# Linear attention and a leaky-ReLU MLP on one core: the two MLP products by one level of Strassen's method

## The chip, the cores and the metric

The kernel runs on one NeuronCore of a Trainium2 chip. The core has a matrix engine (TensorE, PE in the profile; its weight loads are PEld), VectorE (DVE), ScalarE (ACT), GpSimd (POOL) and SyncE (SP), which here issues the loads. Each engine has its own list of instructions and waits for others by semaphores. The metric is the device time of the core in microseconds (us), lower is better.

## The reference, cut to what matters

```python
# q, k, v: (8, 8, 576, 64) f32; g_norm: (64,); w_in: (512, 2048), w_out: (2048, 512), f64
kv  = einsum('bhsd,bhse->bhde', k, v)
out = einsum('bhsd,bhde->bhse', q, kv)
rms = sqrt(mean(out * out, axis=-1, keepdims=True) + 1e-06)
x   = (out / rms * g_norm).transpose(0, 2, 1, 3).reshape(4608, 512)
h   = x @ w_in                      # 4608 x 2048
return maximum(0.01 * h, h) @ w_out # 4608 x 512
```

The weights arrive as float64, seen by the kernel as pairs of 32-bit words; it converts them to float32 itself. All products are in float32.

## The kernel before

The 4608 tokens are worked in nine blocks of 512 (a batch has 576 tokens, so blocks and batches do not coincide). x lies transposed in SBUF: a tile `xT` of a block is 128 partitions x 4 parts (e) x 512 tokens, where a partition and a part together are one of the 512 columns. `w_in` and `w_out` stay in SBUF as `w1` and `w2`.

`mlp` (L225 on in the listing) runs over 16 tiles f of 128 hidden columns. For each, four matmuls of 512 tokens accumulate one h tile in PSUM (L233), ACT writes the leaky ReLU of it to `gT` (L237), and, one tile behind, four matmuls with `gT` as weights add its share to four output accumulators in PSUM (L244), one for each 128 tokens. These are open for the whole block. At the block's end DVE copies them to `o_sb` (L250) and ACT's queue issues the stores (L251). PSUM is full: two h tiles, four accumulators, two attention tiles.

`attention` (L175 on) makes x for one batch and is a generator: `between` (L267) takes one step of it after each f, so it lies between the MLP's matmuls of the block before. Its steps: DVE transposes a pair of heads of q (L181) and PE forms kv (L188); DVE copies kv out (L194) and SP issues the next batch's loads (L71 to L91); then, for each of the two blocks that the batch touches, four o_ps products (L208), ACT's square and scaled copy of each (L210, L211), DVE's sums of squares (L213, L214), a matmul with a 0/1 matrix that adds over a head's columns (L216), the square root on ACT (L219), reciprocal and multiply on DVE (L220, L221). `weights` is a generator too: 32 steps of `round_f64` (L106), each with one 512 KB raw tile from DRAM, two reads of it on ACT (L125, L127) and four instructions on DVE (L128 to L133). Eight of the steps and the whole first attention stand ahead of block 0, the others go two to an f in it. POOL only fills constants at the start.

Within an engine the compiler's scheduler may move instructions; the pools' buffer counts bound how far ahead a load or a tile can run.

Of the kernel before, what the change touches and what calls it, by code (L numbers as in the profile page):

```python
# [21 lines left out]
def kernel(  # L22
# [38 lines left out]
    work = ctx.enter_context(tc.tile_pool(name="work", bufs=2))  # L61
    xpool = ctx.enter_context(tc.tile_pool(name="xpool", bufs=3))
    outp = ctx.enter_context(tc.tile_pool(name="outp", bufs=3))
    ps_att = ctx.enter_context(tc.tile_pool(name="ps_att", bufs=2, space=bass.MemoryType.PSUM))
    ps_h = ctx.enter_context(tc.tile_pool(name="ps_h", bufs=2, space=bass.MemoryType.PSUM))
    ps_o = ctx.enter_context(tc.tile_pool(name="ps_o", bufs=1, space=bass.MemoryType.PSUM))


    loaded = {}

    def load_kv(b):  # L71
        tiles = []
        for name, src in (("k", k), ("v", v)):
            t = ins.tile([P, H, JJ, D], F32, tag=f"{name}_in", name=f"{name}_in", bufs=1)
# [27 lines left out]
    w1_sb = [consts.tile([P, NE, FC * P], F32, name=f"w1_{c}") for c in range(NF // FC)]  # L102
    w2_sb = [consts.tile([P, FC, DM], F32, name=f"w2_{c}") for c in range(NF // FC)]
    w_in_e = w_in.rearrange("(h e i) f -> e h i f", e=NE, i=E)

    def round_f64(dst, srcs):  # L106
# [61 lines left out]
    xTs = {}  # L168
# [135 lines left out]
```

## Time and profile before

| what | value |
|---|---|
| median of three runs | 1196.11 us (1193.37 to 1198.21) |
| the profiled execution | 1196.87 us |
| its span in the trace | 1195.2 us |
| mean granted TensorE clock over the span | 0.972 of full speed |
| PE busy | 1113.5 us in 3488 records |
| read from DRAM / written | 54.27 MB / 9.44 MB |

The trace is of one execution. The span runs from its first to its last recorded work; the execution's own time is 1.7 us longer. Busy time of an engine is a mean over very different stretches, so the rows further down are taken by stretch: the start, in which weights are loaded, the eight blocks behind it, and the end. A group's "idle before" is the time in which that engine had nothing to do just before the group's instructions, with what ended it.

### The profile page before, as it was taken

How to read it: one execution, taken by the hardware profiler on the slowest of the kernel's cores; microseconds unless marked ns; L12 is line 12 of the kernel's file. 1: busy time of each engine (PE TensorE's matmuls, PEld its weight loads, DVE VectorE, ACT ScalarE, POOL GpSimd, SP SyncE). 2: the span in 40 equal slices, each digit the busy share in tenths (PEclk: the TensorE clock that was granted, in tenths of full speed). 3: DMA queues.
4: the chain of work that ended last, by engine and by line, in shares of the span. 5: the costliest groups of instructions: out<-in, count | busy, mean ns of one | idle time of the engine just before them, and what ended most of it. 6: DMA issues, size and time to landing. Idle time of an engine off the chain costs nothing.

```text
span 1195.2 us, 8362 instructions
## 1 busy us (share of the span) xinstructions
PE 1113.5 (93%) x3488; PEld 481.4 (40%) x3488; DVE 201.9 (17%) x277; ACT 184.6 (15%) x354; POOL 2.0 (0%) x9
## 2 busy tenths in 40 slices
PE   1658997999989998999989998999999999999998
PEld 1123432444434443444434443444444344444443
DVE  0663636100020013001300112000400030000000
ACT  0332424100100111011101120011101110000000
POOL 0000000000000000000000000000000000000000
PEclk9779998999999999999989999999999999999999
DMA  8944694700042104040214004400000000000000
GB/s 172 188 113 101 175 198 117 164 0 1 0 114 54 26 0 114 1 80 0 60 54 80 0 1 114 80 0 1 36 1 0 1 36 0 1 0 36 0 1 35
DMA packets 33765, 64.24 MB, mean 54 GB/s; under 512 B 4544, under 2 KB 20928, under 8 KB 33728
## 3 DMA queue, kind: packets, MB, share of 16 engines
q1 hardware_dynamic: 27904, 54.28, 21.2%
q10 hardware_dynamic: 5824, 9.44, 2.2%
q8 instruction: 27, 0.44, 0.2%
q14 instruction: 10, 0.08, 0.0%
HBM read 54.27 MB, written 9.44 MB: 53 GB/s over the span
## 4 chain that ended last, share of the span: by engine, by line
PE 81%; DMA 11%; DVE 4%; SPq 1%; ACT 1%; issue 1%; ACTq 0%; DVEq 0%
PE o_acc L244 39%; PE h_ps L233 36%; DMA q_in<-in_q_dram 5%; PE o_ps L208 3%; DMA out_dram<-o_sb 3%; PE kv_ps L188 1%; DMA raw<-in_moe_w_in_dram 1%; DVE qT L181 1%; DMA raw<-in_moe_w_out_dram 1%; SPq L121 1%; PE ss_ps L216 1%; DVE o_sb L250 1%; DVE tmp L131 1%; DMA k_in<-in_k_dram 0%; DVE w L133 0%
## 5 line engine op out<-in xcount | busy, mean ns | idle before, releaser
L233 PE MATMUL h_ps<-xT,w 128*128 128x512 f32 x1152 | 531.5, 606 | 15.7 <-DVE w L133 15.7
L244 PE MATMUL o_acc<-w,gT 128*128 128x512 f32 x1152 | 526.4, 601 | 17.1 <-ACT gT L237 16.4
L244 PEld LDWEIGHTS o_acc<-w,gT 128*128 128x128 f32 x1152 | 221.1, 193 | 299.4 <-issue 274.0
L233 PEld LDWEIGHTS h_ps<-xT,w 128*128 128x128 f32 x1152 | 215.7, 192 | 284.1 <-issue 260.3
L237 ACT ACTIVATE gT<-h_ps 128x512 f32<-128x512 f32 x144 | 85.5, 596 | 716.8 <-PE h_ps L233 638.7
L181 DVE STREAM_TRANSPOSE qT<-q_in 128x576 f32<-128x576 f32 x32 | 37.5, 1241 | 212.8 <-PE o_ps L208 208.4
L208 PE MATMUL o_ps<-qT,kv 128*32 128x64 f32 (+7 forms) x512 | 56.6, 463 | 13.2 <-DVE qT L181 11.3
L250 DVE COPY o_sb<-o_acc 128x512 f32<-128x512 f32 x36 | 24.0, 686 | 252.5 <-PE o_acc L244 221.9
L210 ACT ACTIVATE sq<-o_ps 128x512 f32<-128x512 f32 (+7 forms) x64 | 26.2, 410 | 203.9 <-PE o_ps L208 203.7
L213 DVE TENSOR_TENSOR sq<-sq 128x1024 f32<-128x1024 f32 (+7 forms) x16 | 12.0, 750 | 233.0 <-ACT sq L210 233.0
L188 PE MATMUL kv_ps<-v_in,k_in 128*64 128x64 f32 (+1 forms) x640 | 32.0, 243 | 17.9 <-DMA v_in<-in_v_dram 17.9
L220 DVE RECIPROCAL rms<-rms 128x512 f32<-128x512 f32 (+7 forms) x16 | 31.2, 1953 | 68.4 <-ACT rms L219 68.4
L194 DVE COPY kv<-kv_ps 64x256 f32<-64x256 f32 x16 | 6.8, 422 | 203.9 <-PE kv_ps L188 203.8
L188 PEld LDWEIGHTS kv_ps<-v_in,k_in 128*64 128x64 f32 (+1 forms) x640 | 25.7, 146 | 38.1 <-issue 35.0
L208 PEld LDWEIGHTS o_ps<-qT,kv 128*32 128x32 f32 x512 | 13.1, 115 | 65.1 <-issue 46.6
L211 ACT ACTIVATE xT<-o_ps,g_sb 128x512 f32<-128x512 f32 (+7 forms) x64 | 31.6, 496 | 0.0
L216 PE MATMUL ss_ps<-sq,same 128*128 128x512 f32 (+7 forms) x32 | 11.1, 431 | 13.6 <-DVE sq L214 13.6
L125 ACT ACTIVATE add<-raw 128x512 uint32<-128x512 uint32 x32 | 21.4, 673 | 12.1 <-issue 8.1
L127 ACT ACTIVATE cut<-raw 128x512 f32<-128x512 f32 x32 | 21.3, 668 | 8.4 <-DVE tmp L131 5.0
L133 DVE CUSTOM_DVE_ANT_0 w<-tmp,add 128x1024 uint16<-128x1024 uint16 x32 | 22.0, 691 | 1.1
L131 DVE SCALAR_TENSOR_TENSOR tmp<-cut,tmp 128x512 uint32<-128x512 uint32 x32 | 21.8, 688 | 0.6
L221 DVE TENSOR_TENSOR xT<-xT,rms 128x2048 f32<-128x2048 f32 (+7 forms) x16 | 21.6, 1352 | 0.2
(16 smaller groups left out, 52.9 us busy)
## 6 DMA issues: line engine op xcount, KB each, us to landing
q_in<-in_q_dram SPq DMA_DIRECT2D x16, 576.0 KB, 11.1
out_dram<-o_sb ACTq DMA_DIRECT2D x36, 256.0 KB, 2.3
q_in<-in_q_dram SPq DMA_DIRECT2D x16, 560.0 KB, 12.7
raw<-in_moe_w_in_dram SPq DMA_DIRECT2D x128, 64.0 KB, 2.5
raw<-in_moe_w_out_dram SPq DMA_DIRECT2D x16, 512.0 KB, 4.7
k_in<-in_k_dram SPq DMA_DIRECT2D x8, 640.0 KB, 6.1
v_in<-in_v_dram SPq DMA_DIRECT2D x8, 640.0 KB, 10.3
k_in<-in_k_dram SPq DMA_DIRECT2D x8, 512.0 KB, 7.9
```

The lines of the kernel that those rows point to most:

```text
L131: nc.vector.scalar_tensor_tensor(tmp, in0=cut.bitcast(U32), scalar=0x80000000, in1=tmp, op0=ALU.bitwise_and, op1=ALU.bitwise_or)
L181: nc.vector.transpose(qT[:, p, :].rearrange("p (t s) -> p s t", s=T), q_in[:, p, :].rearrange("p (s d) -> p s d", d=D)[:, :, :32])
L188: nc.tensor.matmul(kv_ps[64 * l:64 * l + 64, p, :], lhsT=k_in[:n, h, j, :], rhs=v_in[:n, h, j, :], start=(j == 0), stop=(j == JJ - 1))
L208: nc.tensor.matmul(o_ps[32 * p:32 * p + 32, :], lhsT=kv[:, p, e, :, :], rhs=qT[:, p, lo - b * S:hi - b * S], start=True, stop=True)
L210: nc.scalar.activation(sq[:, e, :], o_ps, func=AF.Square)
L211: nc.scalar.activation(x[:, e, :], o_ps, func=AF.Copy, scale=g_sb[:, e:e + 1])
L216: nc.tensor.matmul(ss_ps, lhsT=same.rearrange("p h e -> p (h e)"), rhs=sq[:, 0, :], start=True, stop=True)
L220: nc.vector.reciprocal(rms, rms)
L233: nc.tensor.matmul(h_ps, lhsT=w1_sb[f // FC][:, e, (f % FC) * P:(f % FC + 1) * P], rhs=xT[:, e, :], start=(e == 0), stop=(e == NE - 1))
L237: nc.scalar.activation(gT, h_ps, func=AF.Prelu, alpha=SLOPE)
L244: nc.tensor.matmul(accs[t], lhsT=g_last[:, t * P:(t + 1) * P], rhs=w2_sb[c // FC][:, c % FC, :], start=(c == 0), stop=(c == NF - 1))
L250: nc.vector.tensor_copy(o_sb, accs[t])
```

## The change

Both MLP products are now cut in two along each of their three dimensions, and one level of Strassen's method (in Winograd's form) is applied: seven products of halves where eight stood, with sums of halves before and after. A block stays 512 tokens. The 2048 hidden columns are worked in four chunks c of 512: 256 from the first half and 256 from the second.

- A product is four matmuls of 128x128 weights and 256 columns (two parts of the result times two of the contraction), all into one PSUM bank (`bank`, 128 x 512). There are three banks for h and three for o, named a, b and c; products 1, 6, 7 and 4 share bank a and add up in it, 2 is in b, 5 and 3 share c. The order is 1, 5, 2, 6, 3, 7, 4, and `done` follows each product with the instructions that read it.
- `product_h` and `product_o` are generators over the seven products. Sums of the sides, 128x512 each (`sides_w1`, and `sides_w2` and `sides_g` in the same pattern): for w1 and w2 (`ws1` to `ws4`, `wt1` to `wt4`, made anew in every chunk) and for g (`gs1` to `gs4`) on POOL; for x (`xt1` to `xt4`, once a block) on DVE.
- Results: the first read of a bank is a copy by ACT into a tile of g or o, each later one an addition by DVE of the bank to that tile, and g then gets its ReLU in place by ACT. The outputs `o11` to `o22` are summed in SBUF over the four chunks and stored from there; the open accumulators in PSUM are gone.
- The o products of a chunk run one chunk behind, interleaved with the h products. One step of attention is taken after the second and the fourth product of each five.
- All matmuls keep the order in which they are written (`keep_in_program_order`).
- Partition p and part e of an x tile hold column 4p + e (before, 16 columns in a row of a head lay on 16 partitions of one part), so `w_in` is read by "(p e) f"; a weight step is now one DMA of 512 KB. q, k and v come by pairs of heads with two buffers each, and the raw tiles have two buffers instead of three.

```diff
-    stage = ctx.enter_context(tc.tile_pool(name="stage", bufs=3))
-    conv = ctx.enter_context(tc.tile_pool(name="conv", bufs=2))
+    stage = ctx.enter_context(tc.tile_pool(name="stage", bufs=2))
...
+    def matmul(*args, **kw):
+        tc.keep_in_program_order(nc.tensor.matmul(*args, **kw))
...
+    def load_pair(b, p):
...
+            t = ins.tile([P, 2, JJ, D], F32, tag=f"{name}_in", name=f"{name}_in")
...
-        nc.scalar.dma_start(g_sb[h * E:(h + 1) * E], g_norm.rearrange("(e i) -> i e", i=E))
...
+        nc.scalar.dma_start(g_sb[h * E:(h + 1) * E], g_norm.rearrange("(i e) -> i e", e=NE))
...
-    w_in_e = w_in.rearrange("(h e i) f -> e h i f", e=NE, i=E)
...
+        raw = stage.tile([P, a, n, 2], U32, tag="raw", name="raw")
+        nc.sync.dma_start(raw.rearrange("p a n two -> p a (n two)"), src.bitcast(U32))
...
+    w_in_e = w_in.rearrange("(p e) f -> p e f", e=NE)
+    w_out_u = w_out.rearrange("(h c u p) m -> h c p u m", h=2, c=NC, p=P)
...
+            nxt = (b, p + 2) if p + 2 < NP else (b + 1, p + 2 - NP)
+            if nxt[0] < B:
+                load_pair(*nxt)
...
-            sq = work.tile([P, NE, n], F32, tag="sq", name="sq", bufs=1)
...
-    def mlp(i, xT, between):
...
+    def add(eng, out_, a, b_, minus=False):
+        eng.tensor_tensor(out_, a, b_, op=ALU.subtract if minus else ALU.add)
+    def sides_w1(c):
+        a11, a12 = w1_sb[0][c][:, :2, :], w1_sb[0][c][:, 2:, :]
+        a21, a22 = w1_sb[1][c][:, :2, :], w1_sb[1][c][:, 2:, :]
+        s1, s2, s3, s4 = (wcomb.tile([P, 2, U * P], F32, tag=f"ws{i}", name=f"ws{i}")
+                          for i in range(1, 5))
+        add(nc.gpsimd, s1, a21, a22)
+        add(nc.gpsimd, s2, s1, a11, True)
+        add(nc.gpsimd, s3, a11, a21, True)
+        add(nc.gpsimd, s4, a12, s2, True)
+        return {1: a11, 2: a12, 3: s4, 4: a22, 5: s1, 6: s2, 7: s3}
...
+    def sides_x(x):
+        b11, b12 = x[:, :2, :N2], x[:, :2, N2:]
+        b21, b22 = x[:, 2:, :N2], x[:, 2:, N2:]
+        t1, t2, t3, t4 = (work.tile([P, 2, N2], F32, tag=f"xt{i}", name=f"xt{i}")
+                          for i in range(1, 5))
+        add(nc.vector, t1, b12, b11, True)
+        add(nc.vector, t2, b22, t1, True)
+        add(nc.vector, t3, b22, b12, True)
+        add(nc.vector, t4, b21, t2, True)
...
+    BANK = {1: "a", 6: "a", 7: "a", 4: "a", 2: "b", 5: "c", 3: "c"}
+    def strassen(which, left, right, done):
+        banks = {}
+        for i in (1, 5, 2, 6, 3, 7, 4):
+            first = BANK[i] not in banks
+            if first:
+                banks[BANK[i]] = ps_m.tile([P, 2, N2], F32, tag=f"{which}{BANK[i]}",
+                                           name=f"{which}_{BANK[i]}")
+            bank = banks[BANK[i]]
+            for part in range(2):
+                for r in range(2):
+                    matmul(bank[:, part, :], lhsT=left(i, part, r), rhs=right(i, part, r),
+                           start=first and part == 0 and r == 0, stop=(r == 1),
+                           skip_group_check=True)
+            done(i, bank)
+            yield
...
+        def done(i, bank):
+            if i == 1:
+                nc.scalar.copy(g11, bank)
+            elif i == 5:
+                nc.scalar.copy(g22, bank)
+            elif i == 2:
+                add(nc.vector, g11, bank, g11)
+                relu(g11)
+            elif i == 6:
+                nc.scalar.copy(g21, bank)
+            elif i == 3:
+                add(nc.vector, g21, bank, g21)
+                relu(g21)
+            elif i == 7:
+                add(nc.vector, g22, bank, g22)
+                relu(g22)
+            else:
+                relu(g12, bank)
+                to.append(sides_g((g11, g12, g21, g22)))
...
+        def acc(key, bank, fresh):
+            if c == 0 and fresh:
+                nc.scalar.copy(os[key], bank)
+            else:
+                add(nc.vector, os[key], bank, os[key])
+        def done(i, bank):
+            for key, fresh in {1: [("11", True)], 5: [("22", True)], 2: [("11", False)],
+                               6: [("12", True)], 3: [("12", False)], 7: [("22", False)],
+                               4: [("21", True)]}[i]:
+                acc(key, bank, fresh)
+                if c == NC - 1 and {"11": 2, "12": 3, "22": 7, "21": 4}[key] == i:
+                    finish(key, os[key])
...
+        x_sides = sides_x(xTs.pop(i))
...
+            first = product_h(c, x_sides, g_sides)
+            go(first, 1)
+            go(second)
+            for n in range(5):
+                go(first, 1)
+                go(w_steps, 1)
+                if n in (1, 3):
+                    go(a_steps, 1)
...
+            go(second, 1)
+            go(first)
+            for n in range(5):
+                go(second, 1)
+                go(w_steps, 1)
+                if n in (1, 3):
+                    go(a_steps, 1)
+            before = held
```

In the rows below a name is the tile that the instruction writes, `<-` what it reads, and x4 four alike in a row; the numbers behind names only tell buffers apart. In the changed kernel all matmuls and all additions have a helper's line (L82, L245), so the names tell which they are.

PE in block 1, at the third chunk (before: at the ninth f). Before:

```order
L233 MATMUL h_ps_1536<-xT_895,w1_2_107 128x512 x4
L244 MATMUL o_acc0_1388<-w2_1_110,gT_1523 128x512
L244 MATMUL o_acc1_1389<-w2_1_110,gT_1523 128x512
L244 MATMUL o_acc2_1390<-w2_1_110,gT_1523 128x512
L244 MATMUL o_acc3_1391<-w2_1_110,gT_1523 128x512
L208 MATMUL o_ps_1547<-qT_1396,kv_1_121 32x320 x4
L233 MATMUL h_ps_1554<-xT_895,w1_2_107 128x512 x4
L244 MATMUL o_acc0_1388<-w2_2_111,gT_1541 128x512
L244 MATMUL o_acc1_1389<-w2_2_111,gT_1541 128x512
L244 MATMUL o_acc2_1390<-w2_2_111,gT_1541 128x512
```

Now, from product 1 of h to product 4 of h:

```order
L82 MATMUL h_a_2213<-xT_1070,w1_0_2_118 128x256 x4
L82 MATMUL o_a_2137<-wt4_2128,g22_1872 128x256 x4
L82 MATMUL h_c_2224<-xt1_1853,ws1_2201 128x256 x4
L82 MATMUL h_b_2230<-xT_1070,w1_0_2_118 128x256 x4
L82 MATMUL o_ps_2237<-qT_1897,kv_1_140 32x320 x4
L82 MATMUL h_a_2213<-xt2_1854,ws2_2202 128x256 x4
L82 MATMUL h_c_2224<-xT_1070,ws4_2204 128x256 x4
L82 MATMUL ss_ps_2257<-sq_2116,same_134 128x320
L82 MATMUL h_a_2213<-xt3_1855,ws3_2203 128x256 x4
L82 MATMUL o_a_2277<-w2_0_1_125,g11_2069 128x256 x4
L82 MATMUL h_a_2213<-xt4_1856,w1_1_2_122 128x256 x4
```

Where one h tile and four accumulators took turns, four h products and two o products now take turns by halves, each x4 being one product; bank a is written again and again, and attention's rows stand between products.

DVE at the end of a block with attention. Before, the rest of a batch (reciprocal, multiply) and the output copies:

```order
L220 RECIPROCAL rms_2332<-rms_2332 128x384
L250 COPY o_sb_2340<-o_acc0_2040 128x512
L221 TENSOR_TENSOR xT_2254<-xT_2254,rms_2332 128x4x384
L250 COPY o_sb_2343<-o_acc1_2041 128x512
L250 COPY o_sb_2346<-o_acc2_2042 128x512
L250 COPY o_sb_2349<-o_acc3_2043 128x512
```

Now, the additions to the outputs with a transpose, a reciprocal and a multiply of attention among them:

```order
L245 TENSOR_TENSOR o22_3374<-o_c_3677,o22_3374 128x512
L245 TENSOR_TENSOR o11_3371<-o_b_3683,o11_3371 128x512
L198 STREAM_TRANSPOSE qT_3754<-q_in_3773 128x18x32
L239 RECIPROCAL rms_3691<-rms_3691 128x384
L245 TENSOR_TENSOR o12_3372<-o_a_3658,o12_3372 128x512
L240 TENSOR_TENSOR xT_3546<-xT_3546,rms_3691 128x4x384
L245 TENSOR_TENSOR o12_3372<-o_c_3677,o12_3372 128x512
L245 TENSOR_TENSOR o22_3374<-o_a_3658,o22_3374 128x512
L198 STREAM_TRANSPOSE qT_3754<-q_in_3806 128x18x32
L245 TENSOR_TENSOR o21_3373<-o_a_3658,o21_3373 128x512
```

Additions that free bank a (those that read `o_a`) now stand behind attention's DVE work, where before only the copies at the block's end did.

ACT at the start of the kernel. Before:

```order
L210 ACTIVATE sq_237<-o_ps_238 128x512
L211 ACTIVATE xT_236<-o_ps_238,g_sb_96 128x512
L210 ACTIVATE sq_237<-o_ps_263 128x512
L211 ACTIVATE xT_236<-o_ps_263,g_sb_96 128x512
L210 ACTIVATE sq_237<-o_ps_270 128x512
L211 ACTIVATE xT_236<-o_ps_270,g_sb_96 128x512
L210 ACTIVATE sq_237<-o_ps_288 128x512
L211 ACTIVATE xT_236<-o_ps_288,g_sb_96 128x512
```

Now:

```order
L137 ACTIVATE add_256<-raw_254 128x512
L139 ACTIVATE cut_258<-raw_254 128x512
L227 ACTIVATE sq_273<-o_ps_268 128x512
L228 ACTIVATE xT_267<-o_ps_268,g_sb_107 128x512
L137 ACTIVATE add_278<-raw_276 128x512
L139 ACTIVATE cut_280<-raw_276 128x512
L227 ACTIVATE sq_292<-o_ps_287 128x512
L228 ACTIVATE xT_267<-o_ps_287,g_sb_107 128x512
```

The first squares of attention now stand behind the two reads of the third raw tile, and a further tile's reads stand between them; before, the four tiles of the first attention part were read in a row.

## Rows read from the trace of the kernel before

**Rows 1.** The page: busy us (share) xinstructions of engines; shares of the chain by engine.

```profile
PE 1113.5 (93%) x3488; PEld 481.4 (40%) x3488; DVE 201.9 (17%) x277; ACT 184.6 (15%) x354; POOL 2.0 (0%) x9
...
PE 81%; DMA 11%; DVE 4%; SPq 1%; ACT 1%; issue 1%; ACTq 0%; DVEq 0%
```

**Rows 2.** Windows: stretch, us, each engine's busy us (instructions), clock, DMA share, GB/s.

```profile
0.00:86.40 86.40, 39.79 (x306) 16.40 (x306) 35.77 (x46) 23.19 (x49) 1.97 (x9) 0.85 0.73 157
86.40:226.80 140.40, 124.58 (x377) 53.49 (x378) 71.06 (x125) 46.69 (x83) 0.00 (x0) 0.92 0.68 157
226.80:1190.80 964.00, 949.01 (x2807) 411.51 (x2805) 94.34 (x106) 114.73 (x223) 0.00 (x0) 0.99 0.13 29
1190.80:1195.20 4.40, 0.13 (x1) 0.00 (x0) 0.69 (x2) 0.00 (x0) 0.00 (x0) 0.81 0.48 179
```

**Rows 3.** Chain in order of time: start us, us, engine, tile, line, records.

```profile
274.99 3.43 PE o_acc L244 x8
...
611.32 3.63 PE h_ps L233 x8
```

**Rows 4.** Costliest groups: shapes, records | busy us, mean ns | idle before, releaser.

```profile
L233 PE MATMUL h_ps<-xT,w 128*128 128x512 f32 x1152 | 531.5, 606 | 15.7 <-DVE w L133 15.7
L244 PE MATMUL o_acc<-w,gT 128*128 128x512 f32 x1152 | 526.4, 601 | 17.1 <-ACT gT L237 16.4
...
L208 PE MATMUL o_ps<-qT,kv 128*32 128x64 f32 (+7 forms) x512 | 56.6, 463 | 13.2 <-DVE qT L181 11.3
...
L188 PE MATMUL kv_ps<-v_in,k_in 128*64 128x64 f32 (+1 forms) x640 | 32.0, 243 | 17.9 <-DMA v_in<-in_v_dram 17.9
...
L216 PE MATMUL ss_ps<-sq,same 128*128 128x512 f32 (+7 forms) x32 | 11.1, 431 | 13.6 <-DVE sq L214 13.6
```

**Rows 5.** Timeline of PE, 461.8 to 463.0: start us, us, instruction, records.

```profile
461.93 0.59 PE L216 MATMUL ss_ps<-sq,same 128*128 128x256 f32 x2
462.37 1.02 PE L244 MATMUL o_acc<-w,gT 128*128 128x512 f32 x2
```

**Rows 6.** POOL's groups by line and shape (columns as in rows 4).

```profile
L164 POOL MEMSET kv<- 128x512 f32 x2 | 1.1, 526 | 0.0
L157 POOL TENSOR_SCALAR_AFFINE_SELECT same<-same 128x128 f32<-128x128 f32 x1 | 0.3, 343 | 0.0
```

**Rows 7.** DVE's groups by line and shape.

```profile
L181 DVE STREAM_TRANSPOSE qT<-q_in 128x576 f32<-128x576 f32 x32 | 37.5, 1241 | 212.8 <-PE o_ps L208 208.4 <-DMA q_in<-in_q_dram 4.3
L250 DVE COPY o_sb<-o_acc 128x512 f32<-128x512 f32 x36 | 24.0, 686 | 252.5 <-PE o_acc L244 221.9 <-DMA out_dram<-o_sb 30.4
...
L220 DVE RECIPROCAL rms<-rms 128x384 f32<-128x384 f32 x2 | 5.1, 2553 | 3.3 <-ACT rms L219 3.3
```

**Rows 8.** Timeline at two places, 90 us and 1184 us (columns as in rows 5).

```profile
90.05 0.59 ACT L237 ACTIVATE gT<-h_ps 128x512 f32<-128x512 f32 x1
...
90.69 0.84 PE L244 MATMUL o_acc<-w,gT 128*128 128x512 f32 x1 [0.46 <-ACT gT L237]
...
1183.90 7.03 PE L244 MATMUL o_acc<-w,gT 128*128 128x512 f32 x16
...
1188.39 0.69 DVE L250 COPY o_sb<-o_acc 128x512 f32<-128x512 f32 x1 [106.28 <-PE o_acc L244]
```

**Rows 9.** The page's DMA queues (packets, MB, share) and issues (count, KB, us).

```profile
q1 hardware_dynamic: 27904, 54.28, 21.2%
...
raw<-in_moe_w_in_dram SPq DMA_DIRECT2D x128, 64.0 KB, 2.5
raw<-in_moe_w_out_dram SPq DMA_DIRECT2D x16, 512.0 KB, 4.7
```

**Rows 10.** Waits: engine, line <- waited for: us in total, times, longest us.

```profile
ACT gT L237 <- DMA out_dram<-o_sb: 70.2, 7, 13.1
...
PE o_acc L244 <- ACT gT L237: 16.4, 7, 3.9
```

More of the change, by code (lines that the diff above doesn't have):

```diff
@@ L66 @@
[L66 to L74, printed above, removed]
+    ps_m = ctx.enter_context(tc.tile_pool(name="ps_m", bufs=1, space=bass.MemoryType.PSUM))
+    def matmul(*args, **kw):
+        tc.keep_in_program_order(nc.tensor.matmul(*args, **kw))
+    k_ins, v_ins, q_ins = {}, {}, {}
@@ new lines, with round_f64 @@
+    w1_sb = [[consts.tile([P, NE, U * P], F32, name=f"w1_{h}_{c}") for c in range(NC)]
+             for h in range(2)]
+    w2_sb = [[consts.tile([P, U, DM], F32, name=f"w2_{h}_{c}") for c in range(NC)]
+             for h in range(2)]
+    def round_f64(dst, src):
+        a, n = dst.shape[1:]
+        raw = stage.tile([P, a, n, 2], U32, tag="raw", name="raw")
+        nc.sync.dma_start(raw.rearrange("p a n two -> p a (n two)"), src.bitcast(U32))
+        raw = raw.rearrange("p a n two -> p (a n) two")
@@ L203, in attention @@
             x = block(i)[:, :, lo - i * NT:hi - i * NT]
[L204 removed]
+            sums = None
             for e in range(NE):
@@ new lines, in product_h, with relu @@
+    def product_h(c, x_sides, to):
+        w_sides = sides_w1(c)
+        g11, g12, g21, g22 = (gpool.tile([P, U, N2], F32, tag=f"g{i}", name=f"g{i}")
+                              for i in ("11", "12", "21", "22"))
+        def relu(t, src=None):
+            nc.scalar.activation(t, t if src is None else src, func=AF.Prelu, alpha=SLOPE)
+        def done(i, bank):
[17 more added lines that the diff above has]
+                to.append(sides_g((g11, g12, g21, g22)))
+        yield from strassen("h", lambda i, part, r: w_sides[i][:, r, part * P:(part + 1) * P],
+                            lambda i, part, r: x_sides[i][:, r, :], done)
@@ new lines, in product_o @@
+    def product_o(c, g_sides, os, finish):
+        w_sides = sides_w2(c)
+        if c == 0:
+            for key in ("11", "12", "21", "22"):
+                os[key] = opool.tile([P, 2, N2], F32, tag="o", name=f"o{key}", bufs=6)
+        def acc(key, bank, fresh):
+            if c == 0 and fresh:
+                nc.scalar.copy(os[key], bank)
+            else:
+                add(nc.vector, os[key], bank, os[key])
[6 more added lines that the diff above has]
+                    finish(key, os[key])
+        yield from strassen("o", lambda i, part, r: g_sides[i][:, r, part * P:(part + 1) * P],
+                            lambda i, part, r: w_sides[i][:, r, :], done)
@@ L257, in go, with store, finish @@
             n = None if n is None else n - 1
+    def store(i):
+        def finish(key, o):
+            r0 = i * NT + (int(key[0]) - 1) * N2
+            c0 = (int(key[1]) - 1) * N2
+            nc.scalar.dma_start(
+                out[r0:r0 + N2, c0:c0 + N2].rearrange("(t p) m -> p t m", p=P), o)
+        return finish
     w_steps, a_steps = weights(), attention(0)
-    for _ in range(2 * FC):
+    for _ in range(4):
         go(w_steps, 1)
```

178 lines of the change are left out of this document (88 added, 90 removed).

## The prediction

> **What bounds the kernel now.** I read the page's busy line and chain first [rows 1]: PE is busy 1113.5 of 1195.2 us and holds 81% of the chain; DVE has 17%, ACT 15%, POOL nothing. Then the windows [rows 2], cut at the first h matmul of the first full stretch (86.4), at the first matmul of the second block of tokens (226.8) and at the end of the last matmul (1190.8). The last eight blocks take 964.0 us with PE busy for 949.0 at a granted clock of 0.99, its 2.4 GHz level; the first 226.8 us are different: PE is busy for 39.8 + 124.6 and the DMA engines for 0.73 and 0.68 of the time, at 157 GB/s. Inside the eight blocks the chain [rows 3] is eight records in 3.43 us, again and again, and 3.63 for eight where the stream resumes after the attention's kv matmuls. The code issues 576 matmuls on L233 and as many on L244; the page counts 1152 records of each [rows 4], so one f32 matmul is two passes, 0.429 us each. 2304 passes x 0.429 = 988 us of the span. So the MLP's columns on PE are the bound from 226.8 on, and loading is nearly one before.
>
> **The change, part by part.** *Columns.* 9 blocks x 4 chunks x 2 products x 7 x 4 = 2016 matmuls of 256 columns, 4032 passes. The trace has this very form, 128x128 weights and 256 columns in a running stream: the ss matmul starts at 461.93 and the stream goes on at 462.37 [rows 5], 0.44 for two passes by rounded starts. Half of 0.429 is 0.215; I take 0.216. A product (8 passes) is 1.73 us, all are 4032 x 0.216 = 871 us: 117 us less on PE, nothing beside it.
>
> *Attention on PE* is unchanged: 32.0 + 56.6 + 11.1 us busy for eight batches [rows 4], 12.5 each; with a few of the 0.2 us of resuming [rows 3] I take 13.
>
> *The sums of halves on POOL.* 12 instructions of 128x512 per chunk. No row has a two-input sum on POOL. From below, a 128x512 memset takes 0.53; from above, an affine_select of 128x128 takes 0.34 [rows 6], times four for the columns and times two for the second input 2.7. I take 1.4, the select's rate, nearest in kind. 12 x 1.4 = 17 us lie beside the 24.2 us of a chunk's 14 products. By the order the shortest lead is that of ws1, with seven products (12 us) between h4 and the h5 that needs it, and five POOL instructions in front: 7 us. So POOL costs nothing here; the point from which it does is 24.2/12 = 2.0 us. The Trainium skill (GPSIMD Engine Reference, 3.1 Elementwise) gives 4497 ns for a two-input f32 sum of 2048 elements, by which I estimate 1.1 to 1.2 us here and the same total.
>
> *DVE and ACT.* Per chunk 10 adds on DVE (six in a block's first chunk) at about the 0.69 us of the PSUM copy of the same shape [rows 7], 6.9 us, and 7 instructions on ACT at 0.59 [rows 8], 4.1 us: both lie beside PE. What can reach PE is the reuse of sum "a": product 7 adds into what 6 left, 4 into what 7 left, and in between DVE or ACT must have read it. At four places in a chunk (h6 to h7, h7 to h4, o6 to o7, o7 to o4) only one product, 1.73 us, covers the read. The read's chain: in the last stretch the tenth record of the 16 ends at 1183.90 + 10 x 0.429 = 1188.19 and DVE starts at 1188.39, 0.20; the add, 0.69; and ACT ends at 90.64 and PE starts at 90.69, 0.05 [rows 8]. 0.94 in all, 0.8 to spare. In blocks without attention I count nothing.
>
> *DVE's bursts* use up that spare time. In an attention block's last chunk two transposes of 1.24 [rows 7] stand ahead of the g22 add: after g21 (done 0.9 after h3) they end at 3.4 to 4.0 and the add at 4.1 to 4.7, where PE, with some 0.6 of o_ps, wants h4 at 4.05: 0.1 to 0.6 lost. Later, with 384 columns in the second part, a transpose and a reciprocal of 2.55 stand ahead of o12: 0.9 + 1.24 + 2.55 + 0.69 = 5.4 after o2, where o7 is wanted at 0.65 (ss) + 2 x 1.73 = 4.1: 1.3 lost. The first reciprocal, before g22 in chunk 2, costs 0 to 0.8. With a wait now and then on POOL I take 4 us for each of six attention blocks, 24 us; the bounds are 1 and 10 us a block.
>
> *The first block* ends when the weights are in. Reads are 54.28 MB in all, weights 128 x 64 KB + 16 x 512 KB = 16.8 MB [rows 9], so a batch of q, k and v is 4.69 MB. In the new order of the loads everything but the last four raw tiles (2.1 MB), batches 0 and 1 and half of 2 lie ahead of the last w1 tile's landing: 14.7 + 11.7 = 26.4 MB, at 157 GB/s 168 us. Converting it and the first POOL sum take some 6 us (2 reads on ACT, 4 steps on DVE of 0.4 to 0.7, two sums at 1.4). Then h5 to o7 of chunk 3 remain: 12 products, 20.7, attention 4, waits 4: the second block starts at 203, where it starts at 226.8 now. Attention's first squares stand behind two raw tiles on ACT now, so the first h product comes later than before; but chunks 0 to 2 wait for loads anyway, and the last w1 tile, not that start, sets the end. Bounds: 182 (the same bytes at the 179 GB/s of the last window [rows 2], 147 for 168) and 226.8 (no gain: two raw buffers for three).
>
> *The end.* The last products run without others between: three waits of about 1 us, and 4.4 as now.
>
> *Sum.* At the start of the second block 48 of the 504 products are done. 203 + 456 x 1.73 + 6 x 13 + 24 + 3 + 4.4 = 1101 us of span; the profiled execution took 1.7 more than its span, so 1103, and it stood 0.8 over the median. **Forecast 1102 us**, 7.9% less. The present waits of up to 3.9 us at block ends [rows 10], where ACT's relu stands behind an output DMA, are not in this sum: the first read of h after those DMAs now has four products of cover.
>
> **The rivals.** *POOL becomes the bound.* At 2.7 us, the upper end above, a chunk takes 32.4 us against 24.2 + 3: 32 chunks give 203 + 1037 + 10 = 1250, slower by 4.5%. It turns slower than now from 2.6 us on ((1195 - 213)/32/12). For it: POOL reads two tiles, and every chunk's 12 sums are in one line. Against: the select's 0.34 for 128 columns is the slowest rate that POOL shows, and 2.7 doubles it. 7%.
>
> *The covers are too short.* If each DVE add also waits for one POOL sum of 1.4, the chain is 0.2 + 1.4 + 0.69 + 0.05 = 2.34 against 1.73: 0.6 us at up to four places in 32 chunks, 78 us, 1180; with the bursts at their upper bound (36 more) 1216. For it: POOL is busy more than half of the time. Against: in the trace POOL and DVE never run together, so no row shows such a wait. [...] 7%, mostly near no change.
>
> *Each product pays for its start.* If every change of tile costs the 0.2 us of resuming in [rows 3], 504 x 0.2 = 101 us: 1203, no change. Against: the stream changes from h to o after each eight records and still takes 3.43. 3%.
>
> *The first block gains nothing*: 226.8 for 203, 1126. 14%.
>
> **How the numbers follow.** The forecast with its own spread, 1063 (182 for the first block, 1 us of bursts a block) to 1125: 69%. The other cases as above. The range, 1065 to 1172, leaves out POOL, the upper half of the short covers and the product starts, and the forecast's thin ends. Faster by over 0.5%, about what a measurement of this kernel can tell from no change: 69 + 14 and half of the short covers, 87%; within: 6%; slower: POOL and a part of the covers, 7%.
>
> **What would show it.** Right: records of 256 columns 0.216 apart in every chunk; two blocks without attention at about 97 us each; the second block's first h near 203; POOL busy near 600 us (432 x 1.4) and never ahead of PE in the waits; PE's waits for DVE near 30 us in all, at h4 and o7. Wrong: PE waiting for POOL's ws or gs tiles, a wait at every h4, o4 and o7, or passes of 0.24 and more.

## The result and the profile after

The changed kernel takes 1092.71 us (median of four, 1091.21 to 1094.51) against 1197.03 of the kernel before on the same chip: a ratio of 0.913, 95% interval 0.911 to 0.916. The forecast was 1102. The profiled execution took 1093.87 us, its span 1092.2.

The page of the changed kernel, busy line and chain, to be read beside [rows 1]:

```profile
PE 992.1 (91%) x5216; PEld 808.7 (74%) x5216; DVE 454.0 (42%) x617; ACT 270.9 (25%) x498; POOL 568.9 (52%) x441
...
PE 80%; DVE 10%; DMA 4%; issue 2%; ACT 1%; SPq 1%; ACTq 0%; POOL 0%; DVEq 0%
```

PE still holds the chain, but DVE has more than doubled its work and its share of the chain has risen from 4% to 10%, while the DMA engines' fell from 11% to 4%. Where that lies is in the windows, which I cut at the first h product (59.9), at the first product of chunk 3 (188.6), at the second block's first h (216.0) and around one block without attention (877.5 to 974.2); columns as in [rows 2]:

```profile
0.00:59.90 59.90, 18.84 (x148) 8.13 (x149) 25.63 (x34) 14.13 (x27) 7.98 (x13) 0.79 0.66 170
59.90:120.00 60.10, 43.85 (x240) 33.86 (x239) 36.71 (x61) 23.90 (x41) 21.63 (x17) 0.78 0.63 168
120.00:188.60 68.60, 41.29 (x167) 30.16 (x166) 64.12 (x86) 31.02 (x54) 23.86 (x17) 0.80 0.38 121
188.60:216.00 27.40, 25.96 (x131) 21.47 (x130) 15.73 (x21) 5.46 (x12) 16.68 (x12) 1.00 0.26 65
216.00:877.50 661.50, 654.03 (x3578) 533.13 (x3578) 251.71 (x332) 157.73 (x300) 378.56 (x288) 1.00 0.17 47
877.50:974.20 96.70, 96.70 (x450) 85.10 (x449) 28.98 (x42) 19.34 (x32) 62.19 (x48) 1.00 0.03 12
974.20:1092.20 118.00, 111.39 (x513) 96.82 (x511) 31.14 (x45) 19.33 (x32) 58.00 (x46) 1.00 0.06 19
```

Two readings. A block without attention takes 96.70 us and PE is busy for all of it, with POOL at 62 us beside: 56 products at 1.727. And between 120.0 and 188.6 DVE is busy for 64.1 of 68.6 us, PE for 41.3 and the DMA engines for 0.38: there DVE is the bound, which nothing in the forecast said. The chain in order of time bears it out: of the 64.2 us from 122.6 to 186.8 it spends 55.2 on DVE, 6.2 on ACT and none on PE or on a load. Two of its steps, which took 0.43 and 0.69 us in the kernel before:

```profile
173.87 1.38 DVE tmp L142
175.27 1.65 DVE tmp L143
```

Elsewhere the chain (columns as in [rows 3]) shows the new unit, a product of eight records, and one that follows attention's work:

```profile
104.62 1.73 PE h_a L82 x8
106.34 1.73 PE h_c L82 x8
108.07 0.89 PE o_ps L82 x8
108.96 1.92 PE h_a L82 x8
```

POOL's sums and DVE's additions, and PE's waits for them (columns as in [rows 4] and [rows 10]):

```profile
L245 POOL TENSOR_TENSOR gs<-g,g 128x512 f32<-128x512 f32 x72 | 96.6, 1342 | 51.2 <-ACT g L321 47.9
L245 DVE TENSOR_TENSOR o<-o_a,o 128x512 f32<-128x512 f32 x117 | 80.4, 687 | 143.4 <-PE o_a L82 143.2
...
PE o_a L82 <- DVE o L245: 10.3, 12, 1.3
PE h_a L82 <- DVE g L245: 9.2, 7, 5.8
PE h_c L82 <- POOL ws L245: 6.2, 1, 6.2
```

A sum on POOL is 1.27 to 1.40 us by group, an addition from PSUM on DVE 0.69 as taken. Of PE's own waits one names POOL, 6.2 us in the first block.

**Where the time went.** How much of block 0 is left when block 1 begins differs between the two kernels, so 226.8 and 216.0 cannot be compared as they stand. PE in the kernel before:

```profile
219.90 7.03 PE L244 MATMUL o_acc<-w,gT 128*128 128x512 f32 x16
226.76 7.03 PE L233 MATMUL h_ps<-xT,w 128*128 128x512 f32 x16
```

The sixteen records from 219.90 are the o matmuls of the last two f of block 0, those from 226.76 the first two h tiles of block 1: nothing of block 0 is left, and its first block ends at 226.8. The changed kernel at 216.0 has eight products of block 0 left, 13.8 us: 229.8 in equal terms. So the first block gained nothing, 3 us were lost in it, and the gain lies behind it: 968.4 us there against 862.4, 106 us, of which the columns make 8 blocks x (256 passes x 0.429 - 56 x 1.727) = 8 x 13.1 = 105.

That the two agree so well hides two smaller terms that cancel. The kernel before does most of batch 2's attention already in block 0, where PE has idle time: both batches' kv, 160 records, and 48 of batch 2's 64 records of o_ps. The instructions on o_ps in block 0 and in block 1 (busy us and count on PE, PEld and ACT, then clock, DMA share, GB/s):

```profile
51.60:226.70 175.10, 17.85 (x112) 4.15 (x112) 11.20 (x28) 0.89 0.64 151
226.70:338.30 111.60, 1.07 (x16) 0.32 (x16) 1.28 (x4) 1.00 0.07 19
```

Each of blocks 2 to 6 has 64 of them on PE. So block 1 takes 111.5 us in the kernel before and blocks 2 to 5 take 127.3 to 128.6, while the changed kernel, which keeps its matmuls in order, pays that attention in block 1 (110.7 us, a block without attention 96.7): 12 us that count against it. In its favour, PE's waits at four block ends of the kernel before [rows 10], some 15 us, are gone.

### The profile page after: what moved, and what is told of

The parts are those of the page before. It is cut to its first block, busy times and chain, and to the rows that moved or that the text cites. A ratio compares the mean times of both kernels' runs of the same rounds, so it can differ in the third digit from the quotient of the medians.

```text
span 1092.2 us, 13409 instructions
## 1 busy us (share of the span) xinstructions
PE 992.1 (91%) x5216; PEld 808.7 (74%) x5216; DVE 454.0 (42%) x617; ACT 270.9 (25%) x498; POOL 568.9 (52%) x441
## 4 chain that ended last, share of the span: by engine, by line
PE 80%; DVE 10%; DMA 4%; issue 2%; ACT 1%; SPq 1%; ACTq 0%; POOL 0%; DVEq 0%
PE h_a L82 22%; PE o_a L82 21%; PE h_c L82 11%; PE o_c L82 10%; PE h_b L82 6%; PE o_b L82 6%; PE o_ps L82 3%; DMA k_in<-in_k_dram 2%; PE kv_ps L82 2%; DVE rms L239 2%; DMA raw<-in_moe_w_in_dram 2%; DVE tmp L143 2%; DVE tmp L142 1%; DVE qT L198 1%; DVE o L245 1%
## 5 line engine op out<-in xcount | busy, mean ns | idle before, releaser
L245 POOL TENSOR_TENSOR wt<-w,wt 128x512 f32<-128x512 f32 x72 | 91.7, 1274 | 151.8 <-PE o_a L82 141.5
L82 PE MATMUL o_a<-wt,gs 128*128 128x256 f32 x576 | 142.5, 391 | 6.7 <-DVE o L245 6.7
L82 PE MATMUL h_a<-xt,ws 128*128 128x256 f32 x576 | 141.9, 390 | 0.0
L245 DVE TENSOR_TENSOR o<-o_a,o 128x512 f32<-128x512 f32 x117 | 80.4, 687 | 143.4 <-PE o_a L82 143.2
L82 PEld LDWEIGHTS o_a<-wt,gs 128*128 128x128 f32 x576 | 106.5, 192 | 37.7 <-issue 19.0
L82 PEld LDWEIGHTS h_a<-xt,ws 128*128 128x128 f32 x576 | 106.9, 192 | 28.0 <-POOL ws L245 7.3
L245 POOL TENSOR_TENSOR gs<-g,g 128x512 f32<-128x512 f32 x72 | 96.6, 1342 | 51.2 <-ACT g L321 47.9
L245 POOL TENSOR_TENSOR wt<-w,w 128x512 f32<-128x512 f32 x36 | 46.2, 1283 | 98.1 <-PE o_a L82 98.1
L245 POOL TENSOR_TENSOR ws<-ws,w 128x512 f32<-128x512 f32 x36 | 49.6, 1379 | 85.5 <-PE h_a L82 85.2
L245 DVE TENSOR_TENSOR o<-o_c,o 128x512 f32<-128x512 f32 x63 | 43.5, 691 | 95.4 <-PE o_c L82 89.1
L82 PE MATMUL h_a<-xt,w 128*128 128x256 f32 x288 | 70.8, 390 | 9.2 <-DVE g L245 9.2
L82 PE MATMUL h_a<-xT,w 128*128 128x256 f32 x288 | 71.6, 393 | 7.0 <-DVE w L145 7.0
L245 POOL TENSOR_TENSOR ws<-w,w 128x512 f32<-128x512 f32 x36 | 48.3, 1341 | 56.3 <-DVE w L145 55.6
L82 PE MATMUL h_c<-xt,ws 128*128 128x256 f32 x288 | 69.9, 387 | 6.2 <-POOL ws L245 6.2
L245 DVE TENSOR_TENSOR g<-h_b,g 128x512 f32<-128x512 f32 x36 | 24.9, 692 | 115.4 <-PE h_b L82 115.3
L82 PE MATMUL o_a<-wt,g 128*128 128x256 f32 x288 | 68.3, 380 | 2.9 <-DVE o L245 2.9
L82 PE MATMUL o_ps<-qT,kv 128*32 128x64 f32 (+7 forms) x512 | 49.9, 458 | 22.4 <-ACT xT L228 20.8
L82 PEld LDWEIGHTS h_a<-xt,w 128*128 128x128 f32 x288 | 54.8, 194 | 20.3 <-DVE g L245 13.0
L82 PE MATMUL o_c<-wt,gs 128*128 128x256 f32 x288 | 69.1, 383 | 0.0
L82 PE MATMUL o_a<-w,g 128*128 128x256 f32 x288 | 68.1, 379 | 0.8 <-DVE o L245 0.8
```

The source lines that it names most:

```text
L82: tc.keep_in_program_order(nc.tensor.matmul(*args, **kw))
L245: eng.tensor_tensor(out_, a, b_, op=ALU.subtract if minus else ALU.add)
```

## Experiments

Second block's first h, what of block 0 was left then (in products of 1.727), and the time:

| kernel | first h of block 1 | left | first block in equal terms | median us |
|---|---|---|---|---|
| before | 226.8 | 0 | 226.8 | 1197.0 |
| changed | 216.0 | 13.8 | 229.8 | 1092.7 |
| no_pool | 195.5 | 13.8 | 209.3 | 1071.1 |
| eight | 194.2 | 17.3 | 211.5 | 1175.6 |
| plain0 | 194.8 | 17.3 | 212.1 | 1076.5 |
| plain0_defer3 | 189.5 | 17.3 | 206.8 | 1070.9 |
| stage3 | 215.0 | 13.8 | 228.8 | 1095.2 |
| before_xpe | 181.9 | 0 | 181.9 | 1161.3 |
| split8 | 241.2 | 13.8 | 255.0 | 1120.7 |
| psum0 | 181.4 | 0 | 181.4 | 1045.7 |

My theory behind this result: columns on PE are the gain, POOL is hidden behind the first block, and in the first block POOL's sums slow DVE, which sets the pace there. The rivals: the loads set the first block, POOL or the short covers cost PE everywhere, and a part of the gain is not Strassen's.

### no_pool: the products without sums on POOL

```diff
-        add(nc.gpsimd, s1, a21, a22)
...
-        return {1: a11, 2: a12, 3: s4, 4: a22, 5: s1, 6: s2, 7: s3}
+        return {1: a11, 2: a12, 3: a12, 4: a22, 5: a21, 6: a21, 7: a11}
```

The same in `sides_w2` and `sides_g`. 

> Leaves out all sums on POOL (ws, wt and gs); the products read plain halves of w and g in their place, so the output is not the reference's, and PE has the same 504 products. Theory: in the first block DVE sets the pace from about 120 us on, because its conversion steps that read and write SBUF take longer while POOL adds (the shift L142 0.66 us on average here, 0.425 before). Without POOL they go back to about 0.42 and DVE's other steps to their durations of before, and the second block starts 12 to 20 us earlier than 216, at 196 to 204. Behind it POOL costs PE nothing: the two last full blocks stay at 96.7, the attention blocks at 108 to 110 (110.2 now). Time 1070 to 1082. Rival, the loads set the first block: its end stays within 4 us of 216, time 1086 to 1093. Rival, the sums hold PE up everywhere: the attention blocks fall to 105 or less, time under 1065.

Measured: 1071.09 us; second block at 195.5, 20.5 us earlier (half a microsecond before the expected 196 to 204); attention blocks 109.7 on average for 110.2; the last full block 96.7 as before. The 21.6 us that POOL costs are thus nearly all in the first block. The timeline of the changed kernel there, DVE and POOL from 136 us on:

```profile
136.22 1.50 POOL L245 TENSOR_TENSOR ws<-w 128x512 f32<-128x512 f32 x1 [1.81 <-DVE w L145]
136.62 1.38 DVE L142 TENSOR_SCALAR tmp<-cut 128x512 uint32<-128x512 uint32 x1
137.79 1.33 POOL L245 TENSOR_TENSOR ws<-ws,w 128x512 f32<-128x512 f32 x1
138.03 1.64 DVE L143 SCALAR_TENSOR_TENSOR tmp<-cut,tmp 128x512 uint32<-128x512 uint32 x1
139.20 1.60 POOL L245 TENSOR_TENSOR ws<-w,ws 128x512 f32<-128x512 f32 x1
139.59 0.68 DVE L245 TENSOR_TENSOR o<-o_a,o 128x512 f32<-128x512 f32 x1
140.19 1.16 DVE L145 CUSTOM_DVE_ANT_0 w<-tmp,add 128x1024 uint16<-128x1024 uint16 x1
140.76 1.71 POOL L245 TENSOR_TENSOR wt<-w,w 128x512 f32<-128x512 f32 x1
141.27 1.49 DVE L140 TENSOR_SCALAR cut<-cut 128x512 f32<-128x512 f32 x1
```

and the same four conversion steps without POOL:

```profile
139.63 0.43 DVE L140 TENSOR_SCALAR cut<-cut 128x512 f32<-128x512 f32 x1 [0.20 <-ACT cut L139]
140.09 0.43 DVE L142 TENSOR_SCALAR tmp<-cut 128x512 uint32<-128x512 uint32 x1
140.55 0.69 DVE L143 SCALAR_TENSOR_TENSOR tmp<-cut,tmp 128x512 uint32<-128x512 uint32 x1
141.28 0.69 DVE L145 CUSTOM_DVE_ANT_0 w<-tmp,add 128x1024 uint16<-128x1024 uint16 x1
```

Each conversion step that meets a sum ends shortly after the sum does (L142 at 138.00, the sum at 137.72), so 0.43 becomes 1.38 and 0.69 becomes 1.64; a one-input step (L142, L140) ends 0.3 us after the sum that was running when it began, a two-input step (L143, L145) 0.55. The sums take 1.33 to 1.71 here, for 1.27 where DVE is idle. The addition at 139.59, which has one input in PSUM, takes its 0.68 beside the same sum. The rival that the loads set the first block falls. (The chain gives POOL 0% all the same: what the sums cost appears in it as longer steps of DVE.)

DVE's own work is the other part of that bound: without POOL's sums it is still busy for 45.2 of the 49.4 us from 120.0 to the first product of chunk 3, which now starts at 169.4 for 188.6.

```profile
120.00:169.40 49.40, 35.38 (x155) 26.42 (x156) 45.23 (x77) 27.84 (x50) 0.00 (x0) 0.84 0.44 147
```

The granted clock is a little higher too, 0.84 for 0.80, but PE is not on the changed kernel's chain there.

### plain0: block 0 with eight plain products

```diff
+        x_sides = quarters_x(xTs.pop(0)) if i == 0 else sides_x(xTs.pop(i))
...
+            first = (plain_h if i == 0 else product_h)(c, x_sides, g_sides)
```

> Block 0 by eight plain products (as in the run with eight everywhere), with no sums on POOL and fewer on DVE; blocks 1 to 8 as in the changed kernel; the output is the reference's. Theory: the 20 us by which the first block shrank without POOL's sums (216.0 to 195.5) come from DVE's steps beside POOL, and PE has room for the eighth products there: second block at 194 to 198, two products more outstanding then (3.5 us), the rest unchanged: 1073 to 1079. Rival, leaving the sums out of the later blocks was what gained: 1088 or more.

Measured: 1076.54 us, second block at 194.8. As expected: without the sums block 1 starts as early as in no_pool (195.5), although block 0 now has the eighth products, so PE has room for them there. It is faster than both kernels.

### eight: all of the change but Strassen

```diff
+    EIGHT = (("11", 0, "a"), ("11", 1, "a"), ("12", 0, "b"), ("12", 1, "b"),
+             ("21", 0, "c"), ("21", 1, "c"), ("22", 0, "a"), ("22", 1, "a"))
...
+                           start=(k == 0 and part == 0 and r == 0), stop=(r == 1),
```

> The whole change without Strassen: the same halves, chunks, loads, banks and order of stages, but eight plain products of halves that accumulate in pairs in a bank, and no sums of sides; the output is the reference's. Theory: the gain is the columns alone. 576 products for 504 at 1.727 us are 124 us more, of which 21 lie in the first block beside loads; without POOL's sums the first block is shorter. From a second block at 200 to 216: 521 products x 1.727 = 900, attention 6 x 13, 7 for the ends: 1185 to 1201, no change against the kernel before. Rival, a part of the gain is from the loads by pairs, the whole rows of w_in or outputs that no longer hold PSUM open: 1150 to 1175.

Measured: 1175.56 us, ratio 0.982 (0.980 to 0.985) to the kernel before: 9 us under the expected range, at the edge of the rival. The first block ends 15.3 us earlier in equal terms than in the kernel before, so a part of the change other than Strassen does pay, and Strassen's own part is 1175.6 - 1092.7 = 83 us: 66 products fewer behind the second block's start (522 and 456 left) x 1.727 = 114, less 22 for the later start there and some 10 for DVE's bursts. The blocks also give attention's own price: 122.35 with it, 110.5 without, 11.85 each with hardly a wait.

### before_xpe: the kernel before with x tiles of every fourth column

```diff
-    w_in_e = w_in.rearrange("(h e i) f -> e h i f", e=NE, i=E)
+    w_in_e = w_in.rearrange("(p e) f -> e p f", e=NE)
...
-            jobs = [(w1_sb[c][:, e, :], [w_in_e[e, h, :, cols] for h in range(H)])
+            jobs = [(w1_sb[c][:, e, :], [w_in_e[e, :, cols]])
```

with the same mapping of g and kv. 

> The kernel before with one part of the change alone: x tiles by column 4p + e, so that a raw tile of w_in is one transfer of 512 KB and not eight of 64. Theory: of the 21 us that the plain version with eight products gains on the kernel before, this is a small part: the raw tiles wait for buffers, not for SP's issues (0.44 us each): 1191 to 1197. Rival, the eight issues and short transfers slow the first block: 1180 to 1188.

Measured: 1161.29 us, ratio 0.971 (0.970 to 0.973): 35 us from one mapping, and the largest miss of these runs. A window of the kernel before, and then two of this run:

```profile
60.00:120.00 60.00, 42.99 (x207) 17.86 (x208) 29.95 (x46) 20.00 (x40) 0.00 (x0) 0.84 0.44 109
```

```profile
60.00:120.00 60.00, 56.24 (x188) 24.58 (x189) 43.88 (x82) 28.44 (x48) 0.00 (x0) 0.97 0.79 210
120.00:180.00 60.00, 59.91 (x181) 25.40 (x180) 32.43 (x53) 22.05 (x42) 0.00 (x0) 1.00 0.50 133
```

From 60 us on PE is all but full, where it was busy for 43 of 60; the rate of the loads there is 210 GB/s for 109. So 157 GB/s was not what the transfers could carry. The first block ends 45 us earlier and the kernel only 35: here batch 2's attention lies in block 1 again (all 64 records of o_ps), and that block takes 121.7 us where it took 111.5.

### split8: the changed kernel with eight issues per w_in tile

```diff
-        nc.sync.dma_start(raw.rearrange("p a n two -> p a (n two)"), src.bitcast(U32))
+        pieces = 8 if a == 2 else 1
+        for m in range(pieces):
+            r = slice(m * P // pieces, (m + 1) * P // pieces)
+            nc.sync.dma_start(raw[r].rearrange("p a n two -> p a (n two)"), src[r].bitcast(U32))
```

> The changed kernel with each raw tile of w_in fetched in eight transfers of 16 partitions (64 KB) instead of one, into the same places. Theory: the 35 us that whole transfers gain in the kernel before are the number of issues: 16 tiles x 7 x 0.44 = 49 us more on SP's queue, ahead of everything else that is loaded. Here DVE sets the pace from 120 us on, so less of it is seen: second block at 225 to 250, time 1101 to 1127. Rival, it was the rows' places in DRAM or in SBUF and not the count: within 4 us of 1093.

Measured: 1120.69 us, second block at 241.2. The same bytes to the same places, 28 us slower: the splitting is the cause (more issues, each of them smaller), and not the rows' places. SP's queue in its timeline, first of this run, then of the changed kernel:

```profile
11.29 3.77 SPq L136 DMA_DIRECT2D raw<-in_moe_w_in_dram  x8
83.23 19.27 SPq L136 DMA_DIRECT2D raw<-in_moe_w_in_dram  x32
133.28 15.02 SPq L136 DMA_DIRECT2D raw<-in_moe_w_in_dram  x32
```

```profile
11.30 0.42 SPq L133 DMA_DIRECT2D raw<-in_moe_w_in_dram  x1
77.92 1.15 SPq L133 DMA_DIRECT2D raw<-in_moe_w_in_dram  x2
...
146.22 8.47 SPq L133 DMA_DIRECT2D raw<-in_moe_w_in_dram  x4
```

The first tile holds the queue for 3.77 us in eight issues and for 0.42 in one, so it is the count that the queue pays for. Later four tiles hold it for 15 to 19 us, where two took 1.2 and the last four, with waits for free buffers among them, 8.5; all that is loaded later stands behind them.

### pool16 and pool24: more sums on POOL

```diff
         add(nc.gpsimd, s1, a21, a22)
+        add(nc.gpsimd, s1, a21, a22)
```

For the four sums of w1 (16 a chunk), and for all (24). 

> The four sums of w1 are issued twice, so POOL has 16 instructions a chunk for 12; the output is the reference's. Theory: 16 x 1.33 = 21.3 us a chunk still lie beside 24.2 us of products; blocks behind the first change by under 1 us, the first by up to 6 (DVE is slowed for longer there): 1093 to 1101. Rival, POOL's leads are nearly used up (five instructions stand ahead of the sum that h5 needs), so each chunk pays a good part of the 5.3 us more: 35 chunks x 2 to 5 = 70 to 180, over 1160.

Measured: 1106.23 us. The first block is 8.4 us longer (224.4), the attention blocks 1.1 at most (0.4 on average), the last full one takes 96.8: 16 sums a chunk on POOL are still hidden, and the first block has most of what is lost (10.8 us in the spans, 13.5 in the medians), some 5 more than I allowed.

> Every sum on POOL is issued twice, 24 a chunk; the output is the reference's. Theory: 24 x 1.33 = 32 us a chunk is more than PE's 24.2 (27.6 with attention), so POOL sets the pace: 32 chunks x 32 = 1022 for 855 in the blocks behind the first, and some 10 us more in it: 1255 to 1290. Rival, POOL's instructions are not paid one behind the other, or PE's stream hides them: under 1200.

Measured: 1291.25 us, ratio 1.079, 1 us over the range. A block without attention takes 127.9 us, 32.0 a chunk. Chain and PE's main wait:

```profile
POOL 71%; PE 12%; DVE 9%; issue 3%; DMA 2%; ACT 1%; SPq 1%; POOLq 0%; ACTq 0%; DVEq 0%
...
PE o_c L82 <- POOL wt L245: 107.3, 30, 5.8
```

So the prediction's rival of POOL as the bound is real, and its price for a chunk was right (32.4); 12 sums at 1.32 are 16 us of 24.2, which is why it did not come.

### cover3: bank a read for longer

```diff
+                for _ in range(3 if i in (6, 7, 4) and c > 0 else 1):
                     acc(key, bank, fresh)
```

> In the chunks behind a block's first, each addition of bank a to an output (after o6, o7 and o4) is issued three times in a row, 1.38 us more on DVE each; the sum is then wrong, only the time counts. Theory: a product of 1.73 us covers 0.94 us of reading, 0.8 to spare, so 0.2 + 3 x 0.69 + 0.05 = 2.3 leaves 0.6 uncovered at o6 to o7 and at o7 to o4: 54 places x 0.6 = 31 us, and up to 0.8 more at the places in attention blocks where DVE's bursts have used the spare time: 1123 to 1150. Rival, the covers have nothing to spare: 54 x 1.38 = 75, over 1165. Rival, the reading of bank a is not on PE's path: within 5 of 1092.

Measured: 1155.75 us, 6 us over the range. A block without attention grows by 5.1 us, 0.85 for each of six places where I expected 0.6. One of them, at o7 to o4 (first DVE's line, then PE's):

```profile
947.90 2.14 DVE L245 TENSOR_TENSOR o<-o_a,o 128x512 f32<-128x512 f32 x3 [1.35 <-PE o_a L82]
```

```profile
947.70 1.89 PE L82 MATMUL h_a<-xT,w 128*128 128x256 f32 x8
950.19 1.97 PE L82 MATMUL o_a<-wt,g 128*128 128x256 f32 x8 [0.60 <-DVE o L245]
```

From the covering product's start to the restart are 2.49 us: 0.20 before DVE starts, 2.14 for three additions, 0.15 until PE resumes. With one addition that is 1.04 of 1.73, 0.7 to spare where I had 0.8: the 0.05 I took for the last step, from ACT to PE, was 0.15 here. The cover is short, and enough for one addition.

### stage3, plain0_defer3 and psum0: what the first block could be

stage3 only gives back the third raw buffer (`bufs=3`, four output tiles for six). 

> The changed kernel with three raw buffers as before the change, and four output tiles for six to make the room. Theory: DVE sets the first block's pace from 120 us on, so a third raw tile moves the second block by 0 to 5 us from 216: 1087 to 1093. Rival, two raw buffers hold the loads up: the second block 10 us or more earlier, under 1083.

Measured: 1095.16 us, 2 us over the range, second block at 215.0: raw buffers are not what holds the first block.

plain0_defer3 adds to plain0:

```diff
+            if nxt[0] < B and not (b == 0 and nxt[0] == 1):
                 load_pair(*nxt)
...
+    load_pair(1, 0)
+    load_pair(1, 1)
     second = iter(())
```

> As the run before it in this list, and the first two pairs of batch 1 are loaded behind the first four raw tiles, with three raw buffers (four output tiles instead of six make the room). Theory: 2.3 MB less stand ahead of the first weights, 13 us at 170 GB/s; the first h starts at 46 to 50 where it starts at 59, and 5 to 13 us of it are left at the second block, since DVE and the loads have slack of some 30% there: 1061 to 1072. Rival, the loads behind them set the end whatever their order, or DVE does: within 3 us of the run before it.

Measured: 1070.86 us. The first h starts at 50.2 for 59.1, 5.3 us of it are left at the second block.

psum0 takes the first block as the kernel before had it, with whole transfers, the first two pairs of batch 1 behind six and eight raw tiles, three raw buffers, and the weight tiles in the order in which the f tiles need them:

```diff
+    def first_block(xT, between):
...
+                matmul(accs[t], lhsT=g_last[:, t * P:(t + 1) * P], rhs=w2_sb[h][c][:, u, :],
+                       start=(f == 1), stop=(f == len(tiles)))
...
+        if i == 0:
+            first_block(xTs.pop(0), between)
```

> Block 0 as in the kernel before: 512-column matmuls, outputs accumulated in PSUM and copied once, no sums on POOL and no additions on DVE; weight tiles in the order in which its f tiles need them, the first two pairs of batch 1 behind the first raw tiles, three raw buffers; blocks 1 to 8 as in the changed kernel. The output is the reference's. Theory: DVE's work in the first block, not the bytes, is what the changed kernel and its plain first block pay; the kernel before with whole transfers has its second block at 181.9 with PE at 94 to 100% from 60 us on. So the second block at 178 to 190, with nothing of block 0 left behind it, then 448 x 1.727 = 774, six times 13.5 and 9 for the ends: 1043 to 1057. Rival, the loads by pairs or PE's fixed order hold the first block up: the second block at 200 or later, 1065 or more.

Measured: 1045.73 us, ratio 0.874 (0.873 to 0.875) to the kernel before, 47 us under the changed kernel. Second block at 181.4. Its windows:

```profile
60.00:120.00 60.00, 57.02 (x219) 25.04 (x218) 42.33 (x69) 25.00 (x42) 5.88 (x5) 0.97 0.69 209
120.00:178.00 58.00, 55.51 (x163) 24.07 (x162) 35.45 (x56) 19.55 (x39) 0.00 (x0) 0.97 0.35 104
```

PE is all but full there although it does 256 passes of 512 columns and not seven eighths of them; DVE is busy for 35 of 58 us where it was for 64 of 68.6. This is the fastest version that was run: Strassen where PE is the bound, and the form with little work on DVE where weights are loaded and converted. Several things differ at once from the changed kernel's first block, so the run shows what can be had and not which of them gives it.

## Why the prediction was right where it was, and wrong where it was

Its sum, term by term; attention and waits are 6 x (110.25 - 96.7), and the ends are what remains of the span:

| term | forecast | measured |
|---|---|---|
| second block's first h | 203 | 216.0 |
| 456 products | 788.9 | 787.4 |
| attention and DVE's bursts, six blocks | 78 + 24 | 81.3 |
| the end | 7.4 | 7.5 |
| span | 1101 | 1092.2 |

*Columns: right.* 0.2159 us a pass for 0.216, and nothing beside it. The two ss records [rows 5] were enough to price a form that the MLP did not have.

*POOL: right.* 1.32 us for 1.4, 569 us busy for the 600 named, never ahead of PE behind the first block; 16 a chunk stay hidden and 24 do not. The estimate from the Trainium skill (GPSIMD Engine Reference, 3.1 Elementwise) was 1.1 to 1.2; the rows have 1.27 where DVE is idle.

*The covers: right in kind.* 0.7 to spare for 0.8. PE's waits at products behind the first block (h4, o4, o7, o1) are 10 us in all, 2.5 of them at the end.

*DVE's bursts and attention: 21 us too dear.* Attention costs 11.85 a block on PE, not 13 (7 us for six), and the bursts 1.7, not 4 (14 us). The mechanism is there. At o7 in the last chunk of the block whose reciprocal has 384 columns, with a transpose and that reciprocal ahead of o12, I worked out 1.3 (DVE's lines, then PE's):

```profile
649.67 1.25 DVE L198 STREAM_TRANSPOSE qT<-q_in 128x576 f32<-128x576 f32 x1
650.76 2.49 DVE L239 RECIPROCAL rms<-rms 128x384 f32<-128x384 f32 x1
653.18 0.63 DVE L245 TENSOR_TENSOR o<-o_a,o 128x512 f32<-128x512 f32 x1
```

```profile
653.95 1.97 PE L82 MATMUL o_a<-wt,gs 128*128 128x256 f32 x8 [0.82 <-DVE o L245]
```

It is 0.82 here and 0.9 on average, once a block; the four other waits of the six blocks are 2.1 us together, 0.4 a block, where I had taken 2.7. What is left of the 1.7 is in no wait that the profile names.

*The first block: wrong, in two ways that partly cancel.* The step "the last w1 tile, not that start, sets the end", with 6 us for converting it, failed: the last w1 tile was issued by 155 and chunk 3 starts at 188.6, because DVE was busy for 93% of the 68.6 us before it and held the chain. I had counted conversions and additions on DVE as lying beside PE and the loads, and had not added up DVE's own work in the stretch; and I had priced its steps by rows in which POOL is idle, which the changed kernel's POOL is not. no_pool puts that second part at 20.5 us. The Trainium skill (SBUF — State Buffer, Who interferes with whom) names two cases in which VectorE and GpSimd hold each other off: a VectorE instruction with two SBUF inputs beside a GpSimd instruction that reads SBUF, and a VectorE mode with two ports, open to one-input steps such as tensor_scalar, in which whoever issues first holds the other off for the whole instruction. The rows agree: the two-input step went from 0.69 to 1.64 and the one-input shift from 0.43 to 1.38 (in which mode the shift ran, no row shows). The forecast asked for such waits at the MLP's additions, which have one input in PSUM and showed none, and not at the conversions. The other error went the opposite way: 157 GB/s was read as what the transfers carry, but before_xpe (210 GB/s) and split8 show that issues of 64 KB on SP's queue held it down, and these the change itself removes: the second block of no_pool starts 7.5 us before the 203 of the forecast. A rate that is measured under a limit is no price once the limit is gone.

The rival "the first block gains nothing", at 14%, is what happened in equal terms: with what block 0 leaves behind, it ends at 229.8 for 226.8. (In its own terms, the second block's first h, it said 226.8; that came at 216.0, between the sum's 203 and the rival.) That the total came within 10 us of the forecast is partly luck: attention and bursts gave back 21 us where the first block took 13.

What stays open: the first blocks of before_xpe and psum0 end 25 us before plain0_defer3's in equal terms, and which part of it is DVE's additions and which the order of the loads was not taken apart. Loading by pairs as such is not it: psum0 does so too.

## What to carry to other kernels

Price a stage's engines one by one: an engine that is busy for 17% of a kernel before a change, and for 42% after it, can still be the bound of one stage (93% here). When work is put on an idle engine, look at what the other engines do at that time and whether their steps grow beside it; here additions from PSUM did not and conversions in SBUF did. And an algorithm that saves columns is worth applying only in the stretches where columns are the bound.

## What the runs showed of the hardware that I had not expected

- An SBUF-to-SBUF step on DVE that met a sum on POOL ended only after the sum: a 128x512 shift took 0.43 us alone and 1.38 beside a sum, a two-input step 0.69 and 1.64; a sum on POOL 1.27 alone and up to 2.2 beside DVE. An addition with one input in PSUM stayed at 0.69, the transposes at 1.25 and the reciprocals of 512 columns at 3.35.
- 128 issues of 64 KB in place of 16 of 512 KB cost 28 us in the changed kernel and, with the mapping of the columns, 35 in the kernel before, though the DMA engines were busy for only 0.44 of the time between 60 and 120 us in the kernel before, and 0.79 with whole transfers.
